# A sixth half tile of w1 in the ring, filled by one sequence of loads that stays six ahead

## The chip, the core and the metric

The kernel runs on one core of a Trainium2 chip. The metric is the device time of one execution in microseconds (us). TensorE (PE, with its weight loads shown as PEld), VectorE (DVE), ScalarE (ACT), GpSimd (POOL) and SyncE (SP) each work through their own list of instructions in order and wait for each other by semaphores. SP computes nothing here: every DMA of the kernel is issued from its queue, and a DMA that has to wait holds back all that stand behind it.

## What is computed

The input `x` has 2048 rows of 512 numbers. It is normalised by row (layer norm), goes through attention with 32 heads of 16 numbers, and through a two-layer network; the two are multiplied and added to `x`:

```python
xn  = layernorm(x)
q, k, v = split(xn @ wqkv)                     # 32 heads of 16
s   = softmax(q @ k.T * 16**-0.5) @ v @ wo     # no mask
h   = relu(xn @ w1 + b1) ** 2                  # w1: 512 x 1792
g   = silu(h @ w2 + b2)                        # w2: 1792 x 512
out = x + s * g
```

All matrix operands of the dense parts are held as two numbers, a high and a low part ("split"), and each product is three matmuls. The split of a weight tile is therefore twice as large as the weight itself.

## The kernel before

**The main loop.** After a first stage (layer norm, q, k, v) the kernel runs a loop of 512 *slots*, `st` = 0 to 511. Sixteen slots make a *unit*: four heads by 512 rows of q. In each slot PE does eight matmuls for the attention (four scores for the maxima of a later unit, `max_mm` L288, four scores for the exponentials, L1109) and the products with v of the slot before last (`pv_step`, L361), DVE takes four maxima (L295), ACT four exponentials (L1116). Into the slots a generator, `dense()`, feeds the matmuls of the network: it is the only other work that PE has. All engines' orders in the loop are written out by hand: what the Python code emits first stands first in its engine's list. `later(n, fn)` (L182) emits `fn` at the beginning of the slot n slots further on (`begin`, L1242).

**The network in the loop.** `mlp_tasks` works in eight chunks of 256 rows. A chunk has two phases: 14 output tiles of `xn @ w1` (128 of the 1792 columns each), then the product with w2 (`second`, L540).
- In chunk 0 (`first`, L471) an output tile takes two slots, called a *step* below. w1 comes raw from DRAM into one of three `ex` buffers (`load_w1`, L430), POOL splits it into two half tiles `w1s` (`split_w1`, L438: two instructions for each half, L79 and L80), PE uses them, and two slots later the split halves are written to DRAM (`w1_d`, L444). `ex` also takes the raw w2 tiles from step 9 on (`load_w2`, L456).
- In chunks 1 to 7 (`first_pair`, L502) two output tiles go together in a *pair* of four slots. Their w1, already split, is read back from `w1_d` in four half tiles of 256 KB (`load_parts`, L447, its DMA on L450). The pair's matmuls are issued in 12 units of two, first for one half of the rows (lane 0, first two slots), then all again for the other (lane 1, last two slots); half tile k is read by units 3k to 3k+2 of either lane. `between` (L521 to L526) puts a call behind a unit of lane 1.

**The ring of half tiles.** `ring("w1s")` hands out five buffers in turn. A load into a buffer waits until PE has read what was there. In a pair the first half tile of the next pair is asked for at the beginning (it goes to the fifth buffer), the other three behind units 2, 5 and 8 of lane 1, which free the pair's first three buffers. The half tiles of a chunk's first pair are asked for 15 and 17 slots after its predecessor's second phase began.

**What else is in SP's queue**, by the place s of a slot in its unit (s = 0 is where the maxima of a unit begin; a pair begins at s = 0, 4, 8 or 12): the store and reload of the shifts at s = 1 and 2 (`sh`), the loads of q for the exponentials, six DMAs each at the ends of s = 7 and 8 (`qe`), of q for the maxima, six each at the ends of s = 9 and 11 (`qm`, L133), the sums of a finished unit at s = 10 (`sm`, L379), whose reciprocal DVE takes at s = 13 (L385), their store at s = 14 and the reload as factors (`hl`, L393) at s = 16, POOL's product with them at s = 18 (L399), `on_d` at s = 21. In some units the rows of k (`ka`) or of v for the next four heads come on top.

**POOL's other work.** After two output tiles ACT has written `r` (relu, L485 in chunk 0, L531 later), POOL squares it in place (L488, L534) and splits it into `hT` (L79, L80). `r` has one buffer: the next relu waits until POOL has read it. The one PSUM tile of the network (`pd_t`) waits for the relu in turn.

Of the kernel before, what the change touches and what calls it, by code (L numbers as in the profile page):

```python
# [9 lines left out]
F32R = mybir.dt.float32r  # L10
# [6 lines left out]
P = 128  # L17
# [6 lines left out]
FO = F // P  # L24
# [14 lines left out]
def kernel(  # L39
# [35 lines left out]
    def split(dst, raw, hi_act=False, lo=None):  # L75
        if hi_act:
            nc.scalar.activation(dst[0], raw, AF.Copy)
        else:
            nc.gpsimd.tensor_scalar(dst[0], raw, 1.0, 0.0, op0=ALU.mult, op1=ALU.add)  # L79
        (lo or nc.gpsimd).tensor_tensor(  # L80
            dst[1], raw, dst[0].bitcast(F32), op=ALU.subtract
        )
# [12 lines left out]
    with ExitStack() as ph:  # L95
# [7 lines left out]
        rot = {}  # L103
        turn = {"ka": 0, "qm": 0, "qe": 0, "pt": 0}

        def ring(name):
            t = rot[name][turn[name] % len(rot[name])]
            turn[name] += 1
            return t

        def oldest_first(name):
            n = turn[name] % len(rot[name])
            rot[name] = rot[name][n:] + rot[name][:n]
            turn[name] = 0
# [67 lines left out]
        def later(n, fn):  # L182
            waiting.append((now[0] + n, fn))
# [79 lines left out]
        def terms3(ps, terms):  # L263

            n = len(terms)
            out_ = []
            for t, (lh, rh) in enumerate(terms):
                for i, (a, b) in enumerate(((0, 0), (0, 1), (1, 0))):
                    out_.append((
                        ps,  # L270
                        lambda r, lh=lh, a=a: lh(a, r),
                        lambda r, rh=rh, b=b: rh(b, r),
                        t == 0 and i == 0, t == n - 1 and i == 2,
                    ))
            return out_
# [137 lines left out]
        def mlp_tasks(mp):  # L413
# [8 lines left out]
            wr = m1.enter_context(tc.tile_pool(name="wr", bufs=1))  # L422
            xp = m1.enter_context(tc.tile_pool(name="xc", bufs=1))
            w2t = wp.tile([P, 2, FO, D], F32R, name="w2t")
            rot["w1s"] = [wr.tile([P, 2, 2, P], F32R, name=f"w1s{i}") for i in range(5)]
            turn["w1s"] = 0

            raws = []
# [1 line left out]
            def load_w1(fo):  # L430
                raw = ring("ex").rearrange("p (a b) -> p a b", b=P)
                nc.sync.dma_start(
                    raw, w1[:, fo * P : (fo + 1) * P].rearrange("(ko p) f -> p ko f", p=P)
                )
                raws.append(raw)


            def split_w1(fo):  # L438
                raw, ws = raws.pop(0), [ring("w1s") for _ in range(2)]
                for n, w in enumerate(ws):  # L440
                    split((w[:, 0], w[:, 1]), raw[:, 2 * n : 2 * n + 2])
                state["w"].append(ws)
                later(2, lambda: [
                    nc.sync.dma_start(w1_d[fo, n], ws[n].bitcast(F32)) for n in range(2)  # L444
                ])

            def load_parts(fo, n):  # L447

                w = ring("w1s")
                nc.sync.dma_start(w.bitcast(F32), w1_d[fo, n])  # L450
                if n:
                    state["w"][-1].append(w)
                else:
                    state["w"].append([w])

            def load_w2(fo, n):  # L456
                raw = ring("ex")
                nc.sync.dma_start(raw, w2[fo * P : (fo + 1) * P, :])
                later(n, lambda: split((w2t[:, 0, fo], w2t[:, 1, fo]), raw))

            state = {}

            def load_xc(c):
                    xc = xp.tile([P, 2, KO, CW], F32R, name="xc")
                    for i in range(2):
                        nc.sync.dma_start(
                            xc[:, i].bitcast(F32), xn_d[i, :, :, c * CW : (c + 1) * CW]
                        )
                    state["xc"] = xc

            def first(c, fo):  # L471
                i = fo % 2
                if fo == 0:
                    state["hT"] = hp.tile([P, 2, FO, CW], F32R, name="hT")
                xc, hT, w = state["xc"], state["hT"], state["w"].pop(0)
                ps = pd.tile([P, 512], F32, name="pd_t")[:, :CW]
                if fo + 1 < FO:
                    split_w1(fo + 1)
                if fo + 2 < FO:
                    load_w1(fo + 2)  # L480
                if fo >= FO - 5:
                    load_w2(fo - FO + 5, 3)

                def post():
                    nc.scalar.activation(r[:, i], ps, AF.Relu, bias=b1_t[:, fo : fo + 1])  # L485
                    if i == 0:
                        return
                    nc.gpsimd.tensor_tensor(r, r, r, op=ALU.mult)  # L488
                    fs = slice(fo - 1, fo + 1)
                    split((hT[:, 0, fs], hT[:, 1, fs]), r)  # L490

                return halves(
                    terms3(ps, [
                        (
                            lambda a, q, ko=ko: w[ko // 2][q, a, ko % 2],
                            lambda b, q, ko=ko: xc[q, b, ko],
                        )
                        for ko in range(KO)
                    ]), (12,), post, 2,
                )  # L500

            def first_pair(c, f):  # L502

                if f == 0:
                    state["hT"] = hp.tile([P, 2, FO, CW], F32R, name="hT")
                xc, hT = state["xc"], state["hT"]
                ps = pd.tile([P, 512], F32, name="pd_t")
                mms = []
                for i in range(2):
                    w = state["w"].pop(0)  # L510
                    mms += terms3(ps[:, i * CW : (i + 1) * CW], [
                        (
                            lambda a, q, ko=ko, w=w: w[ko // 2][q, a, ko % 2],
                            lambda b, q, ko=ko: xc[q, b, ko],
                        )
                        for ko in range(KO)
                    ])

                out_, lh, rh, _, last = mms[3 * KO]
                mms[3 * KO] = out_, lh, rh, False, last  # L520
                between = {}  # L521
                if f + 1 < FO // 2:
                    load_parts(2 * f + 2, 0)

                    for k in (1, 2, 3):
                        between[3 * k - 1] = lambda k=k: load_parts(2 * f + 2 + k // 2, k % 2)  # L526

                def post():
                    for i in range(2):
                        fo = 2 * f + i  # L530
                        nc.scalar.activation(  # L531
                            r[:, i], ps[:, i * CW : (i + 1) * CW], AF.Relu, bias=b1_t[:, fo : fo + 1]
                        )
                    nc.gpsimd.tensor_tensor(r, r, r, op=ALU.mult)  # L534
                    fs = slice(2 * f, 2 * f + 2)
                    split((hT[:, 0, fs], hT[:, 1, fs]), r)

                return block(mms, 2, post, between)
# [47 lines left out]
                    yield from halves(mms[36:], (6,), post, 1)  # L586

            load_xc(0)
            load_w1(0)
            load_w1(1)  # L590
            state["w"] = []
            split_w1(0)
            for _ in range(4):
                yield [], None
            for c in range(NCK):
                if c == 1:

                    oldest_first("pt")
                    rot["pt"][:0] = rot["ex"]
                if c == 0:  # L600
                    for fo in range(FO):
                        yield from first(c, fo)
                else:
                    for f in range(FO // 2):
                        yield from first_pair(c, f)
                if c + 1 < NCK:
                    load_xc(c + 1)
                    later(15, lambda: [load_parts(0, n) for n in range(2)])
                    later(17, lambda: [load_parts(1, n) for n in range(2)])
                else:  # L610
                    m1.close()
                    wo_setup()
                for tt in range(CW // P):
                    yield from second(c, tt)
# [453 lines left out]
        for g in range(LEAD):  # L1068
# [19 lines left out]
            if g % 2 and g < 16:  # L1088
                c, i = divmod(g // 2, 2)
# [206 lines left out]
```

## Time and profile before

| | us |
|---|---|
| median of 3 runs | 1710.12 |
| the runs | 1709.32, 1710.12, 1716.56 |
| the profiled execution | 1706.47 |
| its span, first to last instruction | 1704.7 |
| PE busy in the span | 1669.6 |
| DVE busy | 1352.3 |
| ACT busy | 1193.5 |
| POOL busy | 518.9 |

The page of the profile gives busy time by engine and the chain of waits, which is followed back from the last instruction to whatever released each step. Groups of instructions, and the idle time before them with what ended it, can be asked for by tile; a timeline lists instructions with their starts, where rows of the same kind are merged (x6: six of them, with the time from the first's start to the last's end). Windows give the busy time of each engine in a stretch of the span. Times in the rows are us from the span's start unless "ns" is said.

### The profile page before, as it was taken

To read this page: it belongs to the slowest core of one execution; us is meant where nothing else is said; L and a number is where in the kernel's file an instruction comes from. 1 tells how busy PE (TensorE), PEld (TensorE's weight loads), DVE (VectorE), ACT (ScalarE), POOL (GpSimd) and SP (SyncE) were. 2 spreads that over 40 slices of the span, in tenths; PEclk is the share of its full clock that TensorE was granted. 3 is DMA by queue.
4 is the path that set the end of the run, shared out by engine and by line. 5 is a ranking of instruction groups with operands and counts; after the bars stand their busy time and mean duration, and the time that the engine had idled before them with its cause. 6 is when DMAs were issued, how large, how long until landed. Compare 5 with 4: busy or idle time off the path is not lost.

```text
span 1704.7 us, 35480 instructions
## 1 busy us (share of the span) xinstructions
PE 1669.6 (98%) x13312; PEld 948.3 (56%) x13312; DVE 1352.3 (79%) x2299; ACT 1193.5 (70%) x2354; POOL 518.9 (30%) x538
## 2 busy tenths in 40 slices
PE   6999999999999999999999999999999999999998
PEld 5666565556555655565566456545655555555533
DVE  6255588888888888888888888888888888887632
ACT  6221477777777777777777777777777777776675
POOL 4325467513212311231132113311321233134322
PEclk9999999999999999999999999999999999999999
DMA  8665557334422432342343334323432352158434
GB/s 279 196 208 167 172 163 211 97 82 130 129 64 77 134 101 73 102 125 74 81 118 104 81 80 135 114 60 88 134 103 64 87 143 72 47 179 225 126 112 136
DMA packets 156315, 207.73 MB, mean 122 GB/s; under 512 B 50992, under 2 KB 70960, under 8 KB 154608
## 3 DMA queue, kind: packets, MB, share of 16 engines
q1 hardware_dynamic: 156144, 205.46, 41.9%
q8 instruction: 105, 1.72, 0.4%
q14 instruction: 66, 0.54, 0.1%
HBM read 149.04 MB, written 56.08 MB: 120 GB/s over the span
## 4 chain that ended last, share of the span: by engine, by line
PE 91%; DMA 2%; DVE 1%; POOL 0%; ACT 0%; issue 0%; SPq 0%; DVEq 0%; POOLq 0%; ACTq 0%
PE po L361 29%; PE pm_t L288 17%; PE pd_t L235 17%; PE se L1109 12%; PE pd_t L203 9%; PE se L909 4%; DMA w1s<-w_d 2%; PE se L931 1%; DVE mx L295 1%; PE pm_t L1109 0%; PE pm_t L325 0%; PE pm_t L810 0%; ACT pt L1116 0%; PE pd_t L743 0%; SPq L133 0%
## 5 line engine op out<-in xcount | busy, mean ns | idle before, releaser
L295 DVE TENSOR_REDUCE mx<-pm_t 128x1 f32<-128x512 f32 x2048 | 1274.7, 683 | 260.5 <-PE pm_t L288 154.0
L1116 ACT ACTIVATE pt<-se 128x512 f32<-128x512 f32 x1730 | 903.6, 610 | 263.6 <-PE se L1109 226.7
L288 PE MATMUL pm_t<-ka,qm 64*128 64x512 f32 x2048 | 800.0, 424 | 4.7 <-DVE mx L295 4.3
L1109 PE MATMUL se<-qe,ka 64*128 64x512 f32 x2000 | 689.9, 404 | 0.0
L361 PE MATMUL po<-pt,v 128*32 128x512 f32 x3556 | 546.0, 607 | 0.0
L288 PEld LDWEIGHTS pm_t<-ka,qm 64*128 64x128 f32 x2048 | 353.7, 184 | 280.1 <-DVE mx L295 254.0
L1109 PEld LDWEIGHTS se<-qe,ka 64*128 64x128 f32 x2000 | 340.5, 185 | 20.9 <-issue 5.7
L235 PEld LDWEIGHTS pd_t<-xc,w1s 64*128 64x128 f32 x2352 | 292.8, 186 | 90.7 <-issue 82.2
L235 PE MATMUL pd_t<-xc,w1s 64*128 64x256 f32 x2352 | 336.1, 288 | 4.0 <-DMA w1s<-w_d 3.5
L235 PE MATMUL pd_t<-w2t,hT 64*128 64x512 f32 x936 | 259.7, 410 | 0.0
L235 PEld LDWEIGHTS pd_t<-w2t,hT 64*128 64x128 f32 x936 | 156.1, 184 | 73.7 <-issue 65.4
L361 PE MATMUL po<-ex,v 128*32 128x512 f32 x540 | 192.3, 605 | 0.0
L1116 ACT ACTIVATE ex<-se 128x512 f32<-128x512 f32 x270 | 147.6, 613 | 38.4 <-PE se L1109 34.3
L534 POOL TENSOR_TENSOR r<-r 128x512 f32<-128x512 f32 x49 | 51.0, 1041 | 355.9 <-ACT r L531 355.9
L361 PEld LDWEIGHTS po<-pt,v 128*32 128x32 f32 x3556 | 80.0, 108 | 132.8 <-issue 111.2
L553 POOL TENSOR_TENSOR u<-u,b_t 128x512 f32<-128x512 f32 x16 | 20.5, 1284 | 310.2 <-ACT u L552 310.2
L203 PE MATMUL pd_t<-w2t,hT 64*128 64x512 f32 x408 | 105.5, 391 | 0.0
L203 PE MATMUL pd_t<-wot,oc 64*128 64x512 f32 x336 | 90.9, 407 | 2.6 <-DVE m L315 0.8
L399 POOL TENSOR_TENSOR ot<-ot,hl 128x512 f32<-128x512 f32 x30 | 38.5, 1282 | 164.5 <-DMA hl<-r_d 158.6
L203 PEld LDWEIGHTS pd_t<-wot,oc 64*128 64x128 f32 x336 | 58.8, 185 | 46.9 <-DVE mx L295 12.5
L203 PEld LDWEIGHTS pd_t<-w2t,hT 64*128 64x128 f32 x408 | 72.8, 184 | 9.1
L531 ACT ACTIVATE r<-pd_t,b_t 128x256 f32<-128x256 f32 x98 | 41.1, 470 | 51.5 <-PE pd_t L235 51.5
(110 smaller groups left out, 1115.8 us busy)
## 6 DMA issues: line engine op xcount, KB each, us to landing
w1s<-w_d SPq DMA_DIRECT2D x196, 256.0 KB
qm<-q_d SPq DMA_DIRECT2D x384, 32.0 KB
qe<-q_d SPq DMA_DIRECT2D x384, 32.0 KB
ka<-k_d SPq DMA_DIRECT2D x96, 128.0 KB
xn_d<-xT SPq DMA_DIRECT2D x8, 1024.0 KB
k_d<-hl SPq DMA_DIRECT2D x32, 256.0 KB
q_d<-hl SPq DMA_DIRECT2D x32, 256.0 KB
xc<-xn_d SPq DMA_DIRECT2D x16, 512.0 KB
```

Of the source, the lines that this page charges most:

```text
L203: mm = nc.tensor.matmul(out_, lh(r), rh(r), start=first_ and lane == 0, stop=last_ and lane == 1, skip_group_check=True,)
L235: mm = nc.tensor.matmul(out_, lh(r), rh(r), start=first_ and lane == 0, stop=last_ and lane == 1, skip_group_check=True,)
L288: nc.tensor.matmul(ps, qms[u][p][64 * j : 64 * j + 64, qb * P : (qb + 1) * P], kas[qd, p][64 * j : 64 * j + 64, kc * 512 : (kc + 1) * 512] ...
L295: return nc.vector.tensor_reduce(mxs[u][:, c, kc : kc + 1], ps, axis=AX.X, op=ALU.max)
L361: nc.tensor.matmul(po[32 * j : 32 * j + 32, :], vs[qd][:, (4 * kb + j) * VW : (4 * kb + j) * VW + 32], pts[j], start=(kb == 0), stop=(kb = ...
L399: nc.gpsimd.tensor_tensor(ot, ot, hl[:, 1].bitcast(F32), op=ALU.mult)
L531: nc.scalar.activation(r[:, i], ps[:, i * CW : (i + 1) * CW], AF.Relu, bias=b1_t[:, fo : fo + 1])
L534: nc.gpsimd.tensor_tensor(r, r, r, op=ALU.mult)
L553: nc.gpsimd.tensor_tensor(u, u, b2_t, op=ALU.add)
L909: nc.tensor.matmul(out_, lh(slice(0, P)), rh(slice(0, P)), start=first_, stop=last_)
L1109: nc.tensor.matmul(se, kas[qd, j // 2][b : b + 64, kb * P : (kb + 1) * P], qes[u][j // 2][b : b + 64, :], start=True, stop=True,)
L1116: return nc.scalar.activation(pts[j], se, AF.Exp, scale=0.25)
```

## The change

The ring gets a sixth buffer. `load_parts` becomes `load_part`, which takes the next half tile of a running count and asks for it. Before a chunk's first pair six half tiles are asked for, one in each of the slots 14 to 19 after the second phase began; from then on each pair asks for one half tile behind each of the units 2, 5, 8 and 11 of lane 1, so that the load always goes into the buffer which that unit has freed, six half tiles ahead of it. In chunk 0 three raw tiles are loaded at the start instead of two, and a step splits the tile of two steps later and loads that of three steps later. The number of loads, of split instructions and of matmuls stays what it was.

```diff
-            rot["w1s"] = [wr.tile([P, 2, 2, P], F32R, name=f"w1s{i}") for i in range(5)]
+            rot["w1s"] = [wr.tile([P, 2, 2, P], F32R, name=f"w1s{i}") for i in range(6)]
...
-            def load_parts(fo, n):
-
+            def load_part():
+
+                if state["part"] == 2 * FO:
+                    return
+                fo, n = divmod(state["part"], 2)
+                state["part"] += 1
                 w = ring("w1s")
                 nc.sync.dma_start(w.bitcast(F32), w1_d[fo, n])
...
-                if fo + 1 < FO:
-                    split_w1(fo + 1)
                 if fo + 2 < FO:
-                    load_w1(fo + 2)
+                    split_w1(fo + 2)
+                if fo + 3 < FO:
+                    load_w1(fo + 3)
...
-                between = {}
-                if f + 1 < FO // 2:
-                    load_parts(2 * f + 2, 0)
-
-                    for k in (1, 2, 3):
-                        between[3 * k - 1] = lambda k=k: load_parts(2 * f + 2 + k // 2, k % 2)
+
+                between = {k: load_part for k in (2, 5, 8, 11)}
...
-            load_w1(0)
-            load_w1(1)
+            for fo in range(3):
+                load_w1(fo)
             state["w"] = []
             split_w1(0)
+            later(2, lambda: split_w1(1))
...
-                    later(15, lambda: [load_parts(0, n) for n in range(2)])
-                    later(17, lambda: [load_parts(1, n) for n in range(2)])
+                    state["part"] = 0
+                    for k in range(6):
+                        later(14 + k, load_part)
```

## The prediction

> **What bounds the kernel now.** I read the page first, for the chain of waits.
>
> ```profile
> span 1704.7 us, 35480 instructions
> PE 91%; DMA 2%; DVE 1%; POOL 0%; ACT 0%; issue 0%; SPq 0%; DVEq 0%; POOLq 0%; ACTq 0%
> ```
>
> PE is on the chain for 91% of the span. No matmul is added or removed, so the change can only move the waits in front of them. The 2% of DMA are these pieces of the chain in order of time, start and length:
>
> ```profile
> 394.00 4.23 DMA w1s<-w_d
> 599.23 5.58 DMA w1s<-w_d
> 717.47 4.06 DMA w1s<-w_d
> 902.29 3.59 DMA w1s<-w_d
> 1086.26 3.60 DMA w1s<-w_d
> 1201.07 4.70 DMA w1s<-w_d
> 1363.52 4.20 DMA w1s<-w_d
> ```
>
> Their 30.0 us are not what the loads cost, since PE works through most of each piece. The cost shows in windows: the sum over the seven first phases of chunks 1 to 7 (49 pairs), then one pair without a wait and one with the transposition of a shift, and after them the idle time before the users of `w1s` that a DMA ended.
>
> ```profile
> sum 570.61, PE 566.64 PEld 348.39 DVE 495.38 ACT 441.34 POOL 175.94; mean PE 80.95 PEld 49.77 DVE 70.77 ACT 63.05 POOL 25.14
> 706.28:717.67 11.39, 11.39 (x116) 7.06 (x112) 9.92 (x17) 9.22 (x21) 2.92 (x4) 1.00 0.55 142
> 730.84:742.46 11.62, 11.62 (x119) 7.16 (x115) 10.56 (x20) 8.87 (x20) 6.19 (x7) 1.00 0.34 103
> ```
>
> ```profile
>   DMA w1s<-w_d: 11.7, 21
> ```
>
> 49 x 11.39 is 558.1; ten pairs with a shift add 10 x 0.23. So 570.6 - 558.1 - 2.3 = 10.2 us are lost, which agrees with the 11.7 us (there PE and weight loads are added and partly overlap). About 0.8 of it is spread between normal pairs and a first pair that waited for ACT; I count 9.4 us as waits for w1. Chunk 0 has a loss of its own. Steps 9, 11, 12 and 13, of which step 11 is undisturbed:
>
> ```profile
> 259.66:265.68 6.02, 6.02 (x61) 3.72 (x58) 4.97 (x9) 4.55 (x10) 3.08 (x7) 1.00 1.00 299
> 271.73:277.50 5.77, 5.77 (x61) 3.70 (x58) 4.98 (x9) 4.58 (x10) 5.43 (x7) 1.00 0.51 171
> 277.50:283.86 6.36, 6.15 (x60) 3.77 (x56) 5.04 (x9) 4.46 (x9) 6.02 (x8) 1.00 0.67 189
> 283.86:291.26 7.40, 6.51 (x61) 3.78 (x57) 5.26 (x9) 4.95 (x10) 6.39 (x9) 1.00 0.79 218
> ```
>
> 0.25 + 0.59 + 1.63 = 2.5 us. All that the change can win is 9.4 + 2.5 = 11.9 us, 0.7%.
>
> **Why the half tiles come late.** SP's queue ahead of the pair that begins at 717.67, and PE in it:
>
> ```profile
> 701.61 1.74 SPq L450 DMA_DIRECT2D w1s<-w_d  x3
> 703.43 2.94 SPq L133 DMA_DIRECT2D qe<-q_d  x6
> 706.42 0.58 SPq L156 DMA_DIRECT2D v<-v_d  x1
> 707.04 1.53 SPq L450 DMA_DIRECT2D w1s<-w_d  x1
> 708.68 3.61 SPq L133 DMA_DIRECT2D qe<-q_d  x6
> ...
> 713.05 2.62 SPq L133 DMA_DIRECT2D qm<-q_d  x6
> 715.77 0.62 SPq L379 DMA_DIRECT2D sm<-ot  x1
> 716.49 1.83 SPq L450 DMA_DIRECT2D w1s<-w_d  x3
> ```
>
> ```profile
> 704.62 0.28 PE L235 MATMUL pd_t<-xc,w1s 64*128 64x256 f32 x1
> ...
> 717.67 0.50 PE L235 MATMUL pd_t<-xc,w1s 64*128 64x256 f32 x2
> ...
> 718.02 0.40 PE L235 MATMUL pd_t<-xc,w1s 64*128 64x256 f32 x2
> ...
> 718.25 0.40 PE L235 MATMUL pd_t<-xc,w1s 64*128 64x256 f32 x2
> ...
> 719.33 0.38 PE L235 MATMUL pd_t<-xc,w1s 64*128 64x256 f32 x1 [0.47 <-DMA w1s<-w_d]
> ...
> 721.58 0.50 PE L235 MATMUL pd_t<-xc,w1s 64*128 64x256 f32 x2 [0.56 <-DMA w1s<-w_d]
> ```
>
> Three half tiles were asked for at 701.61 as PE freed their buffers. A pair, 11.4 us, later the next three could go at 713.0, but left SP only at 716.49: 18 loads of q at some 0.45 us each, and v, stood before them. The pair's units start 0.35 us after the first and then 0.23 apart, so PE would have read half tile 1 (unit 3) at 718.5; it landed at 719.3. This happens where a pair follows the pair of s = 8 to 11.
>
> **The change, part by part.**
>
> *One half tile further ahead.* Before, three of the four loads of a pair are asked for one pair before their use. Now those behind units 2 and 5 are half tiles 2 and 3 of the next pair, and those behind 8 and 11 are 0 and 1 of the pair after, with a pair more to spare. The loads that can be late are issued first in the group and used one half tile later: three units, 0.7 us. In the pair at 717.67, with the issue unchanged, half tile 2 would land at 719.3 and be used at 719.2: a wait of 0.1 us in place of 1.78 (13.17 us to the next pair's start at 730.84, less 11.39), and half tile 3, one issue behind, lands 0.6 us later (three issues in 1.83 us) and is used 0.7 us later: none.
>
> *The fourth load at the end of lane 1 instead of the start of the pair.* The one at 707.04 goes; a new one stands between 703.35 and the first `qe`. It waits for unit 11, whose last matmul starts at 704.62 and ends at 704.90. SP so leaves at 704.95, and the 21 DMAs behind it start at 705.35 instead of 703.43: 1.9 us later. It gets back the removed issue's normal 0.5, and 0.35 of a wait among the first six `qe` (2.94 us against 2.62 for six `qm`). Of the 1.53 us of the removed issue 1.1 are beyond the normal. Whether they pass on to the next issue behind v, no run shows; elsewhere one `qe` behind v took
>
> ```profile
> 523.58 1.70 SPq L133 DMA_DIRECT2D qe<-q_d  x1
> ```
>
> so I lean to passing on. The group then comes between 0.1 us earlier and 1.05 us later. The wait left is 0.0 to 1.1 us in such a pair. Four are this tight (those of the chain's pieces at 717.47, 902.29, 1086.26 and 1363.52); nearer to the upper end, 0.8 each, that is 3.2 us (ends 0.2 and 4.4). The other waits I take as gone. Gain in chunks 1 to 7: 9.4 - 3.2 = 6.2 us (5.0 to 9.2).
>
> On this the Trainium skill (DMA: Bandwidth & Descriptors, section Issuing engines are not separate DMA queues) speaks the other way: the time a sequencer takes to start a DMA is usually small beside the DMA itself. By it nothing stands long before the half tiles, and the sum would be that of the first rival. The rows of 18 loads of q at 0.45 us each do not agree.
>
> *What else is now behind a wait.* Behind unit 11 also stands, at s = 16, the load of the factors `hl`, up to 1.6 us later than behind unit 8. POOL waits for it already:
>
> ```profile
> POOL ot L399 <- DMA hl<-r_d: 158.6, 15, 24.4
> ```
>
> and then has the rest of the pair (2.92 to 6.19 of 11.4 us busy in the rows above) before the next `r`: nothing. The `sm` load is bounded below (third rival). The later `qm`, `on_d`, `ka` and the six loads of a chunk's start in slots 14 to 19 (before: four in 15 and 17) have several slots to spare: nothing, and a few tenths per chunk if not. The third raw tile at the start is one 256 KB load that stood some 12 us later; only loads of q for later units stand behind it: nothing.
>
> *Chunk 0.* POOL's split of a half tile costs
>
> ```profile
> L79 POOL TENSOR_SCALAR w1s<-ex x28: 400/405/413, 206.1 to 285.5; 128x256 fp32r<-128x256 f32 x28
> L80 POOL TENSOR_TENSOR w1s<-ex,w1s x28: 725/733/744, 206.6 to 285.9; 128x256 fp32r<-128x256 f32 x28
> ```
>
> 0.405 + 0.733, 2.3 us a step, and stays as often. Steps 9 and 12 waited for their own split; it now stands a step earlier: 0.25 + 0.59 us won. In step 13 two waits end, as the chain has it:
>
> ```profile
> 281.23 1.01 POOL r L488
> ...
> 283.02 1.29 POOL hT L80
> ...
> 284.34 0.48 ACT r L485
> ...
> 286.73 0.38 PE pd_t L203
> ```
>
> First the relu waits for POOL to have read `r` (until 284.3), and only then PE for the split (286.73). The second goes. The first stays: before the `r` of steps 10 and 11 POOL's order still has two splits of w1, two of w2 and one set of factors, only each split is a later one. POOL begins that stretch 0.6 us earlier at most, since the `r` of steps 8 and 9 ahead of it comes from ACT, while step 13 is due 0.84 earlier. So about 1.0 of the 1.63 us stays. Won: 0.25 + 0.59 + 0.65 = 1.5 us; ends 0.9 (the relu no earlier) and 2.5 (both waits gone).
>
> **Sum.** 6.2 + 1.5 = 7.7 us, from the profiled 1706.47 to 1698.8. The median of the runs is 3.65 us above the profiled execution; carried over, 1710.1 - 7.7 = 1702.4 us.
>
> **Rivals.**
> 1. *The queue absorbs the fourth load* (the skill's rule, as a mechanism): the over-long issue behind v goes with the load that is removed, groups come as early as now, and chunk 0 wins all. 9.2 + 2.3 = 11.5 us: 1698.6. For it: half of the four loads have 11 us more to spare. Against: the waiting fourth load.
> 2. *The loads stay late* (the change does not do what it says): the whole 1.05 us comes through in every pair after s = 8 to 11, a further pair or two waits, the relu keeps step 13. 4.0 us: 1706.1. For it: the queue is the cause, and no DMA in it goes away.
> 3. *Slower: DVE waits for `sm`.* The load of the sums is issued at 715.77, and its reciprocal stands in DVE's order ahead of the maxima:
>
> ```profile
> 721.71 0.24 DVE L385 RECIPROCAL sm<-sm 128x16 f32<-128x16 f32 x1
> ```
>
> 5.9 us later. The 256 KB pieces above land after 3.6 to 5.6 us, so the 8 KB of sums leave at least 0.3 us, by size more. Beyond that each us is one of PE's, in every unit. It decides from 0.55 us a unit: 30 x 0.55 is 16.3 us, 1718.7. Against it: no wait of DVE for a DMA is on the chain, and the queue before `sm` grows by 1.05 us at most.
>
> **How the numbers follow.** Forecast (5.5 to 9 us won, 1701 to 1704.6) 0.50, rival 1 0.30, rival 2 0.14, rival 3 0.06. 0.5% of 1710.1 is 8.6 us, about what a measurement of this kernel can tell from no change. Faster by more: rival 1 and the edge of the forecast, 0.36. Slower by more: rival 3, 0.06. Within: 0.58. The range takes rival 1 and rival 2 with some spread of the runs: 1697.5 to 1706.8.
>
> **What would show it.** Right: the DMA pieces of the chain shrink from seven to three or four, all in pairs after s = 8 to 11 and at half tile 2; idle time before `w1s` users by DMA falls from 11.7 to 3 or 4 us; step 13 keeps an ACT wait for `hT`, steps 9 and 12 none for `w1s`; the `qe` behind a pair's loads start 1.9 us later. Wrong: no such piece is left (rival 1), pieces of unchanged length (2), idle DVE before the reciprocal (3).

## The result, and the profile after

| | before | after |
|---|---|---|
| median, us | 1712.65 (6 runs) | 1701.62 (6 runs) |
| the runs, us | 1709.32 to 1716.56 | 1697.94 to 1703.13 |
| the profiled execution, us | 1706.47 | 1698.69 |
| its span, us | 1704.7 | 1696.9 |

The ratio is 0.993, with a 95% interval of 0.991 to 0.995: 0.7% faster. The forecast was 1702.4 us, 7.7 us less than the median then known, and 1698.8 us for the profiled execution. Both totals agree with what came. The parts agree less well, as the rest of this section shows.

The page of the changed kernel, its first line and the chain by engine:

```profile
span 1696.9 us, 35477 instructions
PE 91%; DVE 1%; POOL 1%; DMA 1%; ACT 1%; issue 0%; SPq 0%; DVEq 0%; ACTq 0%; POOLq 0%
```

The DMA share of the chain has gone from 2% to 1%. These are all pieces for `w1s` that are left on it, in order of time (start, length):

```profile
716.11 2.88 DMA w1s<-w_d
900.28 2.76 DMA w1s<-w_d
1084.50 2.92 DMA w1s<-w_d
```

Seven pieces have become three. The windows of these three pairs, and the sum over the seven first phases of chunks 1 to 7 (length, then busy time of each engine), in the changed kernel:

```profile
716.58:728.99 12.41, 11.87 (x116) 7.11 (x112) 10.19 (x18) 8.98 (x20) 2.94 (x4) 1.00 0.57 171
900.72:913.04 12.32, 11.85 (x116) 7.12 (x113) 10.19 (x18) 8.98 (x20) 2.94 (x4) 1.00 0.56 168
1084.84:1097.42 12.58, 11.85 (x116) 7.11 (x112) 10.19 (x18) 8.98 (x20) 2.93 (x4) 1.00 0.28 82
...
sum 564.72, PE 562.97 PEld 347.66 DVE 495.43 ACT 441.03 POOL 176.50; mean PE 80.42 PEld 49.67 DVE 70.78 ACT 63.00 POOL 25.21
```

Against a clean pair of 11.39 us they lose 1.0, 0.9 and 1.2 us. The sum was 570.6, so 5.9 us are won here. Above the 560.4 us of 49 clean pairs with their shifts stand now 4.3 us instead of 10.2. In the groups by tile, the idle time before the users of `w1s` that a DMA ended has fallen from 11.7 us in 21 cases to

```profile
  DMA w1s<-w_d: 4.7, 6
```

Chunk 0 did not follow. Steps 3, 9, 12 and 13 of the changed kernel:

```profile
225.41:231.98 6.57, 5.97 (x60) 3.65 (x56) 5.08 (x9) 4.85 (x10) 4.97 (x9) 1.00 0.37 118
260.82:266.57 5.75, 5.75 (x60) 3.71 (x56) 4.96 (x9) 4.55 (x10) 3.10 (x6) 1.00 1.00 292
278.41:284.16 5.75, 5.75 (x60) 3.69 (x57) 4.96 (x9) 4.29 (x9) 5.40 (x8) 1.00 0.54 154
284.16:291.55 7.39, 5.99 (x60) 3.67 (x56) 5.08 (x9) 4.84 (x10) 5.03 (x5) 1.00 0.58 156
```

Steps 9 and 12 are clean (they were 6.02 and 6.36), but step 13 is as long as before (7.40) and step 3, which had no wait, has one of 0.8 us.

**The two totals by stage.** Taken from the starts of the same slots in both traces (after minus before): up to the end of step 0's first slot +0.5 us, the rest of chunk 0's first phase -0.2, from there to the end of chunk 7's first phase -5.7, the rest -2.4: together -7.8. The last stage has no load of w1. In the window below PE does the same work in both kernels, and in the profile of before at a lower granted clock (the number after POOL's busy time). Before, then after:

```profile
1651.40:1657.40 6.00, 5.13 (x27) 2.65 (x28) 1.37 (x3) 2.92 (x6) 0.00 (x0) 0.72 0.00 0
```

```profile
1645.50:1651.50 6.00, 5.12 (x38) 3.44 (x38) 2.20 (x5) 3.30 (x7) 0.00 (x0) 1.00 0.01 3
```

27 matmuls against 38 in 6 us: this stretch took 1.5 us longer. The clock fell there in seven of the twelve kernels' profiles: in all four with the old order of loads, and in three with the new one (fourth_start, q_extra and ring_v below). It did not in the other five, all with the new order. Whether the change has a part in this, twelve single executions do not settle. The prediction had no such term, so the agreement of 7.8 with 7.7 is partly luck: 5.4 us of it lie in the stages that the change touches.

### The profile page after: what moved, and what is told of

It reads as the page before. It is cut to its first block, busy times and chain, and to the rows that moved or that the text cites. A ratio compares the mean times of both kernels' runs of the same rounds, so it can differ in the third digit from the quotient of the medians.

```text
span 1696.9 us, 35477 instructions
## 1 busy us (share of the span) xinstructions
PE 1660.7 (98%) x13312; PEld 944.8 (56%) x13312; DVE 1352.8 (80%) x2299; ACT 1193.1 (70%) x2354; POOL 520.1 (31%) x538
## 4 chain that ended last, share of the span: by engine, by line
PE 91%; DVE 1%; POOL 1%; DMA 1%; ACT 1%; issue 0%; SPq 0%; DVEq 0%; ACTq 0%; POOLq 0%
PE po L361 29%; PE pm_t L288 17%; PE pd_t L235 17%; PE se L1111 12%; PE pd_t L203 9%; PE se L911 4%; PE se L933 1%; DVE mx L295 1%; DMA w1s<-w_d 1%; PE pm_t L1111 0%; PE pm_t L325 0%; ACT pt L1118 0%; PE pd_t L745 0%; SPq L133 0%; PE pm_t L812 0%
## 5 line engine op out<-in xcount | busy, mean ns | idle before, releaser
L553 POOL TENSOR_TENSOR u<-u,b_t 128x512 f32<-128x512 f32 x16 | 20.6, 1288 | 309.4 <-ACT u L552 309.4
```

Source lines behind the costliest of these rows:

```text
L553: nc.gpsimd.tensor_tensor(u, u, b2_t, op=ALU.add)
```

## The experiments

All ratios are to runs of the kernel before on the same chip, with their 95% intervals. "Lost" is the sum over the seven first phases of chunks 1 to 7 above 560.4 us in the profiled execution.

| kernel | median, us | ratio | lost, us |
|---|---|---|---|
| before | 1711 to 1713 | 1 | 10.2 |
| after | 1701.62 | 0.993 (0.991 to 0.995) | 4.3 |
| split_only | 1713.90 | 1.0012 (0.9993 to 1.003) | 18.2 |
| six_buffers | 1706.97 | 0.9966 (0.9949 to 0.9982) | 10.1 |
| ring_only | 1699.59 | 0.9933 (0.9914 to 0.9952) | 6.9 |
| fourth_start | 1697.74 | 0.9926 (0.9903 to 0.9949) | 4.4 |
| q_extra | 1728.60 | 1.0114 (1.0088 to 1.0139) | 24.2 |
| before_v_early | 1708.13 | 0.997 (0.9953 to 0.9987) | 12.3 |
| v_early | 1696.83 | 0.9922 (0.9898 to 0.9946) | 1.7 |
| split_post | 1702.28 | 0.9936 (0.9921 to 0.9951) | 5.8 |
| v_post | 1699.12 | 0.9915 (0.99 to 0.993) | 2.2 |
| ring_v | 1697.46 | 0.991 (0.9895 to 0.9926) | 2.6 |

### Which part does it

**ring_only** is the changed kernel with chunk 0 as before:

```diff
-                if fo + 2 < FO:
-                    split_w1(fo + 2)
-                if fo + 3 < FO:
-                    load_w1(fo + 3)
+                if fo + 1 < FO:
+                    split_w1(fo + 1)
+                if fo + 2 < FO:
+                    load_w1(fo + 2)
...
-            for fo in range(3):
-                load_w1(fo)
+            load_w1(0)
+            load_w1(1)
             state["w"] = []
             split_w1(0)
-            later(2, lambda: split_w1(1))
```

> Chunk 0 as before, the ring of six and the six-ahead loads as in the changed kernel. Theory (two independent parts): chunks 1 to 7 win the 6.2 us that the changed kernel wins there, and the three waits behind the loads of v stay (1.0, 0.9 and 1.2 us); chunk 0 waits in steps 9, 12 and 13 as before (0.25, 0.6, 1.6 us) and has no wait in step 3. Against before about 6 us less. Rival (the sixth buffer alone already frees the splits of chunk 0): no wait in steps 9 and 12, about 7 us less.

**split_only** is the kernel before with these lines the other way round, and the ring cut to five after chunk 0:

```diff
+                if c == 0:
+                    oldest_first("w1s")
+                    rot["w1s"] = rot["w1s"][:5]
```

> Only the part in chunk 0: three raw tiles at the start, split two ahead in six buffers; after chunk 0 the ring is cut to five and the pairs load as before. Theory: the waits of steps 9 and 12 go (0.85 us won), a wait of 0.8 us comes in step 3 where POOL stands at the split of the fourth raw tile ahead of r, step 13 keeps 1.6 us: within 0.5 us of before, and all seven waits of chunks 1 to 7 as before. Rival (the wait in step 3 is an accident of the one profiled run, an SP instruction of 1.99 us): no wait in step 3, 0.9 us won.

The ring alone has the whole gain (0.9933), the split two ahead alone has none (1.0012). In the profile of ring_only chunk 0 waits in steps 12 and 13 (0.4 and 1.6 us) as expected, but not in step 9; the three waits behind v are there and lost 1.0, 0.7 and 3.4 us, the last with a lowered clock (last section).

Step 3 of split_only has no wait: there the rival was right, and the wait in the changed kernel is not a fixed cost of the split two ahead. In SP's queue of the changed kernel, two stores of a split tile stand ahead of the load of the fourth raw tile:

```profile
214.50 2.45 SPq L444 DMA_DIRECT2D w_d<-w1s  x2
217.00 0.43 SPq L432 DMA_DIRECT2D ex<-in_B_w_dram  x1
```

One of the two took 1.99 us, where most take 0.3 to 0.5. The tile landed at 220.3, POOL split it ahead of `r`, and the relu of step 2 waited for POOL. In v_early and fourth_start, which have the same chunk 0, step 3 loses no more than 0.2 us. In q_extra (below), which puts more issues ahead of that tile, it loses 1.8 us.

Split_only shows a second thing. From chunk 1 on it asks for its half tiles exactly as the kernel before does, but its seven first phases are

```profile
sum 578.58, PE 569.85 PEld 349.27 DVE 495.89 ACT 441.59 POOL 176.77; mean PE 81.41 PEld 49.90 DVE 70.84 ACT 63.08 POOL 25.25
```

against 570.6 in the profile of before: 8 us more lost with the same loads, 3.2 of them as longer busy time of PE. So the profile of before was probably a lucky execution (1706.47 us; of 52 timed runs of this kernel two are faster), and the waits that the ring removes cost more in most others. That would explain why the medians differ by 11 us and the profiles by 7.8; only these two executions of the loads were compared.

**six_buffers** is the kernel before with one number changed:

```diff
-            rot["w1s"] = [wr.tile([P, 2, 2, P], F32R, name=f"w1s{i}") for i in range(5)]
+            rot["w1s"] = [wr.tile([P, 2, 2, P], F32R, name=f"w1s{i}") for i in range(6)]
```

> The kernel before with a sixth buffer in the ring and nothing else: the loads stay where they were (one at a pair's start, three behind units 2, 5 and 8), each into a buffer that has been free for some time. Theory (what helps is the order, one half tile more ahead at the place where SP's queue is late): the groups behind s = 8 to 11 are as late as before, the waits in chunks 1 to 7 stay between 9 and 17 us, as in the two executions of these loads seen so far; within 2 us of before. Rival (a free buffer lets the loads leave earlier): waits below 6 us, 4 us or more less than before.

By its profile the theory holds (10.1 us lost), by its time it does not: 5.5 us less than before (0.9966). So a free buffer alone does help. The profile does not show where: it has six pieces of the chain for `w1s`, where before had seven and split_only ten. About half of the gain each is what the medians say (1712.5, 1707.0, 1699.6); the intervals of the last two kernels touch, so the shares are not settled.

### What makes the half tiles late

**v_early** is the changed kernel with the load of v four slots earlier:

```diff
-            if st % 64 == 48 and st // 64 + 1 < NQ:
+            if st % 64 == 44 and st // 64 + 1 < NQ:
```

> The changed kernel with the load of v four slots earlier (s = 4 instead of 8), out of the stretch in which 18 loads of q stand. Theory (the three waits left are those of v and of the long instruction behind it, 0.6 + 1.6 to 2.1 us in SP's queue): no wait at half tile 2 in the three pairs, 3.1 us less than the changed kernel. Rival 1 (the 18 loads of q alone make them late): waits of 0.8 us or more stay. Rival 2: the waits move to the pairs in which v now stands, no gain.

The sum of its seven first phases, and the idle time before users of `w1s` that a DMA ended:

```profile
sum 562.12, PE 562.12 PEld 347.58 DVE 494.93 ACT 440.69 POOL 176.60; mean PE 80.30 PEld 49.65 DVE 70.70 ACT 62.96 POOL 25.23
```

```profile
  DMA w1s<-w_d: 0.4, 2
```

PE is busy in all of the 562.1 us. The three waits are gone, 2.6 us in this view where 3.1 were expected, and no other came. Its median is 4.8 us below that of the changed kernel, with overlapping intervals.

**q_extra** puts three small loads that nobody reads ahead of the six loads of q at s = 9:

```diff
+            if s == 9 and in_loop:
+                for n in range(3):
+                    x = sp.tile([16, 16], F32, name=f"x{n}", bufs=1)
+                    nc.sync.dma_start(x, q_d[0][0, :DH, 16 * n : 16 * n + 16])
             if s in (9, 11) and u + 1 < NU:
```

> The changed kernel with three more loads of 1 KB into tiles that nobody reads, ahead of the loads of q for the maxima at s = 9: three more places of 0.42 to 0.46 us in SP's queue in every unit. Theory (lateness is the sum of what stands ahead in the queue): the group behind s = 8 to 11 leaves 1.3 us later; the three waits behind v grow from about 1.0 to about 2.3 us each, the other pairs behind s = 8 to 11, which have 1.4 to 1.6 us to spare, start to wait up to 0.3 us: 4 to 6 us more than the changed kernel. Rival (what makes the three late is the long instruction behind v, and SP catches up): the waits stay at about 1 us, within 1 us of the changed kernel.

The pairs that answer to the first, second and third of the changed kernel, and the sum of the seven first phases:

```profile
727.60:743.52 15.92, 13.43 (x117) 7.77 (x113) 10.19 (x18) 8.98 (x20) 2.93 (x4) 0.89 0.50 140
915.18:928.85 13.67, 11.76 (x116) 7.09 (x112) 10.10 (x18) 8.89 (x20) 2.85 (x4) 1.00 0.54 160
1101.72:1115.40 13.68, 11.92 (x118) 7.16 (x114) 10.19 (x18) 8.98 (x20) 2.94 (x4) 1.00 0.25 80
```

```profile
sum 584.56, PE 570.52 PEld 350.02 DVE 496.09 ACT 441.94 POOL 176.40; mean PE 81.50 PEld 50.00 DVE 70.87 ACT 63.13 POOL 25.20
```

In the second and third pair 12.32 and 12.58 became 13.67 and 13.68: 1.35 and 1.10 us for three issues that move 3 KB. There lateness is the length of the queue, as the theory had it. The total was far from the 4 to 6 us expected. The first pair went from 12.41 to 15.92: PE waits 2.5 us in it and then runs at a lowered clock (last section). The first phases lost 20 us more in all, because other pairs began to wait too, two of them losing 4.2 and 4.9 us (at 448.61 and 1379.52) in the same way. Another 12 us were lost outside the first phases, 5.4 of them before chunk 1 and 6.5 behind chunk 7.

**before_v_early** makes the edit of v_early in the kernel before.

> The kernel before with only the load of v moved from s = 8 to s = 4: ring of five, loads as before. Theory (lateness is the sum of what stands in SP's queue before the group): the waits at 717.67, 902.49 and 1087.26 (1.75, 1.28 and 1.40 us in the profile of before) fall to 0.3 us or less, since 2.2 us or more leave the queue; the waits without v (0.4 to 1.9 us) stay: 4 us less than before. Rival (with one pair to spare the loads are late anyway): each of the three keeps 1 us, less than 1.5 us won.

The waits of the three pairs are gone, and the median is 5.3 us below before (0.997), 4 expected. The profiled execution lost 12.3 us all the same, 5.7 of them in one pair, without v, which had lost 0.6 in the profile of before. Moving one DMA in SP's queue is worth half of what the changed kernel brings.

### The fourth load

**fourth_start** asks for a pair's fourth half tile where the kernel before has a load, at the start of the next pair:

```diff
-                between = {k: load_part for k in (2, 5, 8, 11)}
+                between = {k: load_part for k in (2, 5, 8)}
+                if f:
+                    load_part()
```

> The changed kernel with the fourth load of a pair asked for at the start of the next pair instead of behind unit 11. Theory (the fourth load holds the queue behind it for 1.9 us, as predicted): the q loads start 1.9 us earlier, one instruction of 0.4 to 0.5 us comes in again, the group behind v leaves about 1.4 us earlier and its three waits of 0.9 to 1.2 us go: 3 us less than the changed kernel. Rival (the long instruction behind v passes on to the load at the pair's start, or the queue refills): the group leaves less than 0.5 us earlier, waits of 0.5 us or more stay.

SP's queue ahead of the first of the three pairs, in the changed kernel (pair at 716.58) and in fourth_start (pair at 719.40):

```profile
700.50 3.64 SPq L454 DMA_DIRECT2D w1s<-w_d  x4
704.19 2.74 SPq L133 DMA_DIRECT2D qe<-q_d  x6
706.98 0.58 SPq L156 DMA_DIRECT2D v<-v_d  x1
707.65 4.37 SPq L133 DMA_DIRECT2D qe<-q_d  x6
...
712.53 2.76 SPq L133 DMA_DIRECT2D qm<-q_d  x6
715.38 0.62 SPq L379 DMA_DIRECT2D sm<-ot  x1
716.11 1.83 SPq L454 DMA_DIRECT2D w1s<-w_d  x4
```

```profile
703.33 1.74 SPq L454 DMA_DIRECT2D w1s<-w_d  x3
705.16 2.94 SPq L133 DMA_DIRECT2D qe<-q_d  x6
708.15 0.57 SPq L156 DMA_DIRECT2D v<-v_d  x1
708.76 1.73 SPq L454 DMA_DIRECT2D w1s<-w_d  x1
710.60 3.91 SPq L133 DMA_DIRECT2D qe<-q_d  x6
...
718.60 1.37 SPq L454 DMA_DIRECT2D w1s<-w_d  x3
```

Counted from the pair's start the q loads begin 1.8 us earlier (14.2 ahead of it instead of 12.4), but the group leaves only 0.3 us earlier (0.8 ahead instead of 0.5). The 1.5 us between are lost again to the extra issue (0.5), to a wait among the first six `qe` (0.2) and to long issues, of which there are two (1.73 and one within the 3.91) instead of the one of 2.06 within the 4.37. The waits are 1.3, 0.35 and 0.7 us, and 1.0 in the pair at 1362.49: no 3 us won. The rival was right. The place of the fourth load makes no difference that these profiles or the ratios show.

### Step 13, and the combinations

**split_post** moves the split and the raw load of chunk 0 behind the step's post work:

```diff
-                if fo + 2 < FO:
-                    split_w1(fo + 2)
-                if fo + 3 < FO:
-                    load_w1(fo + 3)
 
                 def post():
                     nc.scalar.activation(r[:, i], ps, AF.Relu, bias=b1_t[:, fo : fo + 1])
-                    if i == 0:
-                        return
-                    nc.gpsimd.tensor_tensor(r, r, r, op=ALU.mult)
-                    fs = slice(fo - 1, fo + 1)
-                    split((hT[:, 0, fs], hT[:, 1, fs]), r)
+                    if i:
+                        nc.gpsimd.tensor_tensor(r, r, r, op=ALU.mult)
+                        fs = slice(fo - 1, fo + 1)
+                        split((hT[:, 0, fs], hT[:, 1, fs]), r)
+                    if fo + 2 < FO:
+                        split_w1(fo + 2)
+                    if fo + 3 < FO:
+                        load_w1(fo + 3)
```

> The changed kernel, in chunk 0 POOL's split of w1 and the raw load behind it are put behind the post work of the step (relu, r, hT) instead of ahead of it. Theory (the wait of step 13 is POOL's order: two splits stand ahead of r): the relu of step 12 finds r read, the wait of 1.6 us in step 13 falls below 0.3 us, chunks 1 to 7 unchanged: 1.5 us less than the changed kernel. Rival (POOL's whole work is the bound from step 9 on): the wait moves to the splits of steps 12 and 13, less than 0.5 us won.

Step 13 waited 2.0 us instead of 1.6: the relu still for `hT`, and then PE for the split, which now came last. The theory fell, the rival holds. **v_post** is v_early with this edit, **ring_v** is v_early with chunk 0 as before.

> The changed kernel with v early and with the splits of chunk 0 behind the post work. Theory (two independent places): no wait for w1 in chunks 1 to 7 and none over 0.3 us in step 13: about 1.3 us less than with v early alone, 4.5 us less than the changed kernel. Rival: as for the run before, no gain over v early alone.

> The ring of six with six-ahead loads and v early, chunk 0 as before the change. Theory (the split two ahead is worth nothing that can be measured): within 2 us of v early with the new chunk 0, no wait for w1 in chunks 1 to 7. Rival (the split two ahead gives its 0.9 us and saves more in undisturbed executions): 2 us or more slower than it.

v_post also has 2.0 us in step 13. Of chunks 1 to 7 it has one wait, 1.3 us in the pair at 1357.54, ring_v two of 0.3 and 0.7 us. The medians of v_early, v_post and ring_v (1696.8, 1699.1, 1697.5) are not told apart by their intervals. All three beat the kernel before by 0.8 to 0.9%. Ring_v is the one with the fewest edits: the ring of six, six ahead, v four slots earlier.

## Why the prediction was right, point by point

- **One half tile further ahead: right.** The pieces that are left on the chain are all at half tile 2, all in pairs behind s = 8 to 11, as said, and three of them. The gain in the first phases was put at 6.2 us and measured 5.9.
- **The fourth load and the queue: right, with the terms a little off.** The q loads begin 12.4 us ahead of the pair instead of 14.2, 1.85 us later (1.9 said), the long issue passes on to the `qe` behind v (0.8 us more there, 1.1 said), the first six `qe` give back 0.2 us (0.35 said), and the group comes 0.7 us later, within the -0.1 to +1.05 given. Of the four waits of 0.8 us three came, at 1.0, 0.9 and 1.2, the last above the 1.1 given as the most. The fourth, in the last chunk, did not come in this execution, but came with 1.0 us in fourth_start and 1.7 in split_post. That 3.1 us stayed where 3.2 were said is luck in part: three waits were larger, and one was missing.
- **The rule of the Trainium skill, as a rival.** That starting a DMA costs a sequencer little beside the DMA (the Trainium skill, DMA: Bandwidth & Descriptors, section Issuing engines are not separate DMA queues) is not what this queue shows. In q_extra three more issues of 1 KB in each unit took the changed kernel from 1701.6 to 1728.6 us. From start to start the 1 KB loads took 0.46 us each (median), the same as the 32 KB loads of q. The measurement decides: one such issue may be little, but what counts for these half tiles is how many stand ahead.
- **Chunk 0: wrong.** 1.5 us were to be won, 0.2 were: steps 9 to 13 took 30.7 us instead of 31.6, and step 3 lost 0.8. The step that failed is "POOL begins that stretch 0.6 us earlier at most", with "about 1.0 of the 1.63 us stays". The rows where the stretch begins, with the issue of the raw tile that is split there, and the end of the stretch, before:

```profile
259.73 0.44 SPq L432 DMA_DIRECT2D ex<-in_B_w_dram  x1
```

```profile
263.77 0.41 POOL L79 TENSOR_SCALAR w1s<-ex 128x256 fp32r<-128x256 f32 x1 [2.69 <-PE pm_t L288]
```

and after:

```profile
260.91 0.45 SPq L432 DMA_DIRECT2D ex<-in_B_w_dram  x1
```

```profile
264.90 0.41 POOL L79 TENSOR_SCALAR w1s<-ex 128x256 fp32r<-128x256 f32 x1 [2.42 <-PE pd_t L203]
...
284.23 1.27 POOL L80 TENSOR_TENSOR hT<-r,hT 128x512 fp32r<-128x512 f32 x1
```

  POOL starts 4.1 us after step 9 has begun in both kernels (259.66 and 260.82). The rows name PE, but the semaphores in the traces say otherwise: POOL is held until 263.66 by the load issued at 259.73, which lands at 263.63, and after the change until 264.80 by the one issued at 260.91, which lands at 264.76. The prediction took `r` for what stands ahead and left the raw tile out. The edit asks for a raw tile one step earlier and splits it one step earlier, so there is still one step between the two. From there POOL works without a pause up to the end of `hT`, 20.5 us before (to 284.3) and 20.6 after (to 285.5). The relu of step 12 cannot come earlier than that. What steps 9 and 12 no longer waste is waited for in step 13. Only the second wait there, for the split, is won: 0.9 us (the lower end given), in split_only 0.8.

  The other profiles with this chunk 0 fit. The stretch takes 20.5 to 20.7 us in each. It begins 3.5 us behind the start of step 9 in v_early, 5.2 in fourth_start and 5.3 in q_extra, each time as a raw tile lands, and steps 9 to 13 take 30.2, 33.4 and 33.3 us. The last two are longer than before, with a lowered clock behind the wait in step 13. No run asked for the raw tiles earlier, so this cause is read from the traces and not tried. In split_post these splits come earlier, POOL waits for the relu until 265.7 instead, works on from there, and step 13 is no shorter.
- **"The third raw tile at the start ...: nothing": right.** Step 0 of the changed kernel waits 1.4 us for the first split, and that of before did not. But ring_only, with two raw tiles, waits 1.3 there, and before_v_early 1.6, while split_only, with three, does not wait. In the profile of before PE ran at a clock of 0.57 in the 8 us ahead and came later, as this window shows (the clock stands behind POOL's busy time):

```profile
199.00:207.00 8.00, 7.85 (x36) 2.81 (x34) 6.32 (x12) 5.71 (x11) 0.81 (x2) 0.57 0.92 262
```

  In split_only it was 0.53 to 0.61 there. Step 3's wait of 0.8 us is told above.
- **Slower because DVE waits for `sm`: not in chunks 1 to 7.** In the tail of the changed kernel one such piece is on the chain (1.90 us at 1550.76), but the kernel before has the same one (1.90 us at 1556.66), so the change has no part in it. The prediction's "no wait of DVE for a DMA is on the chain" overlooked it. Its 30 x 0.55 is 16.5 us, not 16.3, and the 1718.7 has the 7.7 us of the forecast already taken off.
- **The sum.** 7.7 us said. 5.9 and 0.2 were won in the places named, 0.5 went the other way at the start, and most of the rest of the 7.8 is the clock late in the span. That the medians moved by 11 us was not foreseen: the prediction read the size of the waits from one execution, and the same loads cost 10.2 us in that and 18.2 in split_only's.

## What to carry to other kernels

Where one queue issues everything, count the instructions between the event that frees a buffer and the load that fills it. A load that is asked for early is late if twenty small ones stand ahead of it, and moving one of these can be worth as much as another buffer. Waits on the same loads differed by almost a factor of two between two executions here, so judge a change that removes them by several runs, and read from the profile where they are, not how much they cost. And work that fills an engine without a pause sets its own end: waits taken away ahead of that end come back there.

## What the runs showed of the hardware that was not expected

**Long issues go with instruction loads.** Most DMA issues on SP take 0.3 to 0.45 us, a few 0.9 to 2.6. In the changed kernel there are 29 over 0.9 us between 330 and 1450 us, of 1210. Seven stand directly behind a load of v. Each of the other 22 has a packet of the instruction queue (q8) in it or at most 0.6 us ahead of it. There are 77 such packets in the stretch, so three or four of the 22 would meet one by chance. In the kernel before it is 26 of 26, and over all twelve profiles 306 of 331, where chance would give some 45. Around the issue of 2.06 us behind v, the DMA queues of the changed kernel from 707.6 to 709.8 (packets, MB, share):

```profile
q1 hardware_dynamic: 1089, 0.31, 69.9%
q8 instruction: 1, 0.02, 4.1%
```

That the one causes the other was not tried.

**A long wait can cost more than itself.** The pair of before_v_early that lost 5.7 us, from the wait on (length, busy times, and the granted clock behind POOL's):

```profile
1200.30:1203.00 2.70, 1.66 (x18) 1.06 (x14) 2.28 (x4) 2.12 (x5) 2.11 (x3) 1.00 1.01 313
1203.00:1206.00 3.00, 0.97 (x9) 0.77 (x9) 0.99 (x2) 1.06 (x2) 0.00 (x0) 1.00 0.91 202
1206.00:1209.00 3.00, 2.84 (x12) 0.95 (x14) 0.00 (x0) 0.03 (x1) 0.00 (x0) 0.53 0.05 18
1209.00:1212.00 3.00, 3.00 (x27) 1.80 (x29) 2.09 (x4) 1.58 (x3) 0.00 (x0) 0.90 0.00 0
```

PE waits about 3.2 us in three pieces, the longest 1.96, and then runs at 0.53 of its clock for 3 us. In ring_only a wait of 1.0 us in the pair at 1083.57, with one of 0.2 us behind it, was enough:

```profile
1086.50:1089.60 3.10, 2.90 (x19) 1.17 (x19) 0.93 (x3) 1.08 (x2) 0.00 (x0) 0.79 0.20 44
1089.60:1092.60 3.00, 3.00 (x22) 1.52 (x18) 1.97 (x3) 1.16 (x3) 0.00 (x0) 0.65 0.13 45
```

while the waits in the changed kernel, in which PE idles for 0.5 to 0.7 us, had no such sequel (clock 1.00 in the three windows above). The length of a wait alone does not decide: in q_extra single waits of 1.9 and 1.8 us (the pairs at 915.18 and 1101.72) left the clock at 1.00, and the three longest, of 2.2, 2.5 and 2.9 us, were each followed by 3.4 us at half of it. What else decides is open. The Trainium skill (TensorE: Matmul & The Clock Gate, section HAM oscillation — how this bites in real kernels) gives the rule that PE shouldn't idle for more than about 3.4 us; here the clock fell behind shorter waits.
